# Four steps of an attention stage issued at other units: reciprocal sums, mask ranks, weight shifts, v loads

## The chip, the cores and the metric

One core of one Trainium2 chip. The metric is device time of the whole program in microseconds (us), the median of several runs. One execution was also recorded by the hardware profiler; all rows below come from that one. The engines are TensorE (PE), VectorE (DVE), ScalarE (ACT), GpSimd (POOL) and SyncE (SP), which here only issues DMAs.

## The reference

Three layers in a chain: clustered attention over 2 x 8 heads of 768 tokens with 64 dimensions, then a 512-2048-512 layer with a rational activation over 1536 tokens, then a 512-1024-512 layer with h * softmax(h) and a layer norm.

```python
q_assign = argmax(q_n @ c_n);  k_assign = argmax(k_n @ c_n)        # 16 clusters per head
scores = where(q_assign == k_assign, scale * q @ k.T, -1e9)
attn = softmax(scores);  x = attn @ v                               # heads side by side
h = x @ w_in;   P = a0 + a1*h + a2*h2 + a3*h3;   Q = 1 + |b0||h| + |b1|h2
x = (P / (Q + 1e-6)) @ w_out
h = x @ w2_in;  solu = h * softmax(h);  out = layernorm(solu) * g_ln @ w2_out
```

The weights arrive as 64-bit floats, whose two words the kernel turns into 32-bit floats itself.

## The kernel before

**Units.** The attention runs over 16 heads (n = 0 to 15) of six units each (t = 0 to 5), 96 units in all; a unit is 128 queries against 768 keys. `unit_scores` puts the scores in one of two PSUM tiles (two pairs of matmuls, L370 with q1/k1, L376 with q2/k2, the second carrying low parts and 16 mask rows). `unit_max` reduces them on VectorE (L381), `unit_exp` takes the exponential on ScalarE (L394), and every second unit `turn_p` transposes two units' probabilities on VectorE (L411). `pv_step` (L421) multiplies them with v one head later, 64 matmuls in each of the units t = 3, 4, 5. So a unit's scores can start only when the exponential of the unit two before has freed its PSUM tile.

**Beside the units** go four kinds of work, each cut into steps that the loop issues at chosen units:

- `prep_head(n+1)` on GpSimd: five operations (L324 three times, L338, L343) that split q and k of the next head, and two DMAs that copy its mask rows (L347, L348).
- `assign` for sets 2, 3 and 4 of heads: similarities on TensorE (L243), a copy on ScalarE (L252), then eight steps: `to_token` (L286), `top` (L290), `is_top` (L294), `rank` on GpSimd (L269), `top`, `is_top`, `from_token` (L297), `mask_out` (L304). The table `TCH` gives their units counted from `AT` = 5, 27, 50.
- `w1_f32`: ten half tiles of weights are turned from 64-bit to 32-bit, each a DMA (L116), a scaling on ScalarE (L126), a shift on VectorE (L127) and a shift-and-or on VectorE (L129), spread over units 28 to 87. This text calls one such half tile a conversion.
- for each pair of heads, `pair_sums` (the reciprocal of the sums, written to DRAM as rd, L463, and read back spread over partitions as rb, L466) and `pair_fin` on GpSimd (one add, L473, and two products with rb, L487).

All DMA issues named here stand in one queue, SyncE's, in one order; a DMA that waits holds those behind it. `load_head(n+2)`, called in the first unit of head n, loads q and k of a later head (dup) and its v. The v tile has two buffers, and v of head n+2 takes the one of head n, which `pv_step` reads in head n+1.

**The order on each engine** is not the order of the Python calls: the tile framework's scheduler sets it from those calls and its own timing estimates, so a moved call can move neighbours too. On each engine instructions then run in that order.

Of the kernel before, what the change touches and what calls it, by code (L numbers as in the profile page):

```python
# [15 lines left out]
B, H, S, D = 2, 8, 768, 64  # L16
# [14 lines left out]
def fused_kernel(ctx: ExitStack, tc: tile.TileContext, qT, kT, v, cent, w1, w2i, w2o, gln, coef, centT, cst, out):  # L31
# [20 lines left out]
    def psum1(name):  # L52
# [35 lines left out]
    S1A, S1B = 3, 7  # L88
    AT = (0, 0, 5, 27, 50)
    TCH = {  # L90
# [3 lines left out]
    }  # L94

    OLAG = 2
# [14 lines left out]

    def to_f32(w, src, nm):
        raw = cv[0].tile([128, 512], mybir.dt.uint64, name=f"raw{nm}", tag="raw")
        nc.sync.dma_start(out=raw, in_=src)  # L116
        yield
        words = raw.bitcast(U32).rearrange("p (n two) -> p n two", two=2)
        lo, hi = words[:, :, 0], words[:, :, 1]
        wf, wu = w, w.bitcast(U32)  # L120

        nc.scalar.activation(out=wf, in_=hi.bitcast(F32), func=AF.Prelu, scale=2.0 ** -112, alpha=-(2.0 ** 32))  # L126
        nc.vector.tensor_scalar(wu, wu, 3, None, op0=ALU.logical_shift_left)  # L127
        yield
        nc.vector.scalar_tensor_tensor(wu, lo, 29, wu, op0=ALU.logical_shift_right, op1=ALU.bitwise_or)  # L129
        yield  # L130
# [5 lines left out]
    w1_f, w1_t = {}, {}  # L136

    def w1_f32(f):
        w1_f[f] = wl0.tile([128, 1024], F32, name=f"w1f{f}", tag="l")
        for a in range(2):  # L140
            o = slice(512 * a, 512 * a + 512)
            yield from to_f32(w1_f[f][:, o], w1[f, :, o], f"w1{f}{a}")

    def w1_parts(f):
        h = wh["l" if f in (0, 12) else "r" if f < 5 or f > 12 else "m"].tile([128, 1024], F32R, name=f"w1h{f}", tag="h")
# [10 lines left out]
            yield  # L156


    raw = {}
    last = {}  # L160

    def load_pairs(es, parts=1):
# [12 lines left out]
    def load_head(n):  # L175
        b, h = divmod(n, H)
        for i, src in enumerate((qT, kT)):
            t = qk.tile([128, S], F32, name=f"dup{n}{i}", tag=f"dup{i}", bufs=2)
            if n:
                nc.sync.dma_start(out=t[0:64], in_=src[b, h])  # L180
            nc.sync.dma_start(out=t[64:128], in_=src[b, h])
            raw["d", n, i] = t

        t = qk.tile([128, S // 32, D], F32, name=f"v{n}", tag="v", bufs=2)
        for r in range(4):
            nc.sync.dma_start(out=t[32 * r:32 * r + 32], in_=v[b, h])
        raw["v", n] = t


    sets = [[(0, 0), (0, 1)], [(1, 0), (1, 1)], [(2, 0), (3, 0), (2, 1), (3, 1)], [(4, 0), (5, 0), (4, 1), (5, 1)], [(6, 0), (7, 0), (6, 1), (7, 1)]]  # L190
# [7 lines left out]
    t = psum4("warm")  # L198
# [108 lines left out]
    NB = 2  # L307
    q1 = [None] * NB
    q2, k1, k2 = [None] * NB, [None] * NB, [None] * NB
    vv = {}  # L310
    for i in range(NB):
        q1[i] = qk.tile([128, S], F32R, name=f"q1{i}", tag=f"q1{i}", bufs=1)
        q2[i] = qk.tile([128, S], F32R, name=f"q2{i}", tag=f"q2{i}", bufs=1)
# [16 lines left out]
    def prep_head(n, er=None, es=None):  # L330
        er = er or nc.gpsimd
        es = es or nc.gpsimd
        b, h = divmod(n, H)
        i = n % NB
        a, c, w = raw.pop(("d", n, 0)), raw.pop(("d", n, 1)), raw.pop(("v", n))
        rnd(er, k1[i], c, sgn[:, 1:2])
        yield
        es.tensor_tensor(k2[i][0:64], c[0:64], k1[i][0:64].bitcast(F32), op=ALU.subtract)  # L338
        yield
        rnd(er, q1[i], a, sgn[:, 0:1])  # L340
        rnd(er, q2[i][0:64], a[0:64], -0.125)
        yield
        es.tensor_tensor(q1[i][64:128], a[64:128], q1[i][64:128].bitcast(F32), op=ALU.subtract)  # L343
        yield
        if n:
            assert masked[next(k for k, es in enumerate(sets) if (n // 2, 0) in es)] == S
            nc.sync.dma_start(out=q2[i][64:80].bitcast(F32), in_=mk.pop((n, 0)).bitcast(F32))  # L347
            nc.sync.dma_start(out=k2[i][64:80].bitcast(F32), in_=mk.pop((n, 1)).bitcast(F32))  # L348
        yield
        vv[n] = w  # L350

# [10 lines left out]
    def unit_scores(n, t):  # L362
        i = n % NB
        sp = psum2("s", f"s{n}_{t}")
        sl = slice(t * 128, (t + 1) * 128)
        before = None
        for f in pre.pop(n * NT + t, ()):
            before = f(sp) or before
        for a in range(2):
            r = nc.tensor.matmul(sp[:, a, 0:384], lhsT=q1[i][:, sl], rhs=k1[i][:, a * 384:(a + 1) * 384], start=True, stop=False)  # L370
            if a == 0:
                last["pe0"] = r
            if before:
                behind(r, before)
        for a in range(2):
            last["pe"] = nc.tensor.matmul(sp[:, a, 0:384], lhsT=q2[i][:, sl], rhs=k2[i][:, a * 384:(a + 1) * 384], start=False, stop=True)  # L376
        return sp
# [114 lines left out]
    plan, planc, planp = ([[] for _ in range(97)] for _ in range(3))  # L492

    def spread(gen, n, i0, i1, plan=plan):
        for i in range(n):
            plan[min(96, i0 + (i1 - i0) * i // n)].append(gen)
# [5 lines left out]
    def run_plan(i):  # L502
        with tc.issue_after(last["pe"].ins) if i < 6 else ExitStack():
            for g in plan[i]:
                next(g, None)
        for h, p in ((("dve", "act"), planc), (("act",), planp)):
            with ExitStack() as es:
                for e in h:
                    es.enter_context(tc.issue_after(last[e].ins))
                for g in p[i]:  # L510
                    next(g, None)
# [24 lines left out]
    for i, (x1, x2, er) in enumerate(((q1[0], q2[0], nc.gpsimd), (k1[0], k2[0], nc.vector))):  # L536
        c, x = raw["p", 0, i], raw.pop(("d", 0, i))
# [4 lines left out]
        else:  # L542
            rnd(er, x2[0:64], c[0:64], -0.125)
            er.tensor_tensor(x1[64:128], x[64:128], x1[64:128].bitcast(F32), op=ALU.subtract)
    vv[0] = raw.pop(("v", 0))
    sps = [psum2("s", f"sim0{a}") for a in range(2)]
    for a in range(2):
        sims(0, 3 * a, 3, sps[a][:, 0, 0:384])
# [19 lines left out]
    for a in range(2):  # L568
        c = slice(384 * a, 384 * a + 384)
        nc.scalar.activation(out=q2[0][64:80, c], in_=ts[a][0:16, 0:384], func=AF.Identity, scale=-BIG, bias=big[0:16])  # L570
    for a in (1, 0):
        c = slice(384 * a, 384 * a + 384)
        nc.vector.tensor_copy(k2[0][64:80, c], ts[a][32 * jk:32 * jk + 16, 0:384])  # L573
    for a in range(2):
        c = slice(384 * a, 384 * a + 384)
# [39 lines left out]
    for idx, (n, t) in enumerate(units):  # L615
        if idx == ACL:
            asg.close()
            wh["r"] = ctx.enter_context(tc.tile_pool(name="wh2", bufs=4, side="right"))
        for k in range(3, len(sets)):
            if idx == AT[k] - LD:  # L620
                load_pairs(sets[k])
        if t == 0:
            if n + 2 < B * H:
                load_head(n + 2)
            if n >= 1 and n + 1 < B * H:
                spread(prep_head(n + 1), 7, idx, idx + 6)
        sp = unit_scores(n, t)
        m = unit_max(n, t, sp)
        if t % 2 and idx > 1:
            turn_p(*divmod(idx // 2 - 1, NT // 2))  # L630
        if idx == S1A:
            set1_a()
        if idx == S1B:
            set1_b()

        if n and t >= 3:
            for i in range(4 * (t - 3), 4 * (t - 2)):
                pv_step(n - 1, i)
            if t == 5 and n % 2 == 0:
                pair_sums(n // 2 - 1)  # L640
        unit_exp(n, t, sp, m)
        if n >= 2 and t < 2:
            pv_out(n - 2, t)
            if t == 1 and n % 2:
                spread(pair_fin(n // 2 - 1), 8, idx + 1, idx + 5)
        run_plan(idx)
    for i in range(2):
        pv_out(B * H - 2, i)
# [9 lines left out]
        pass  # L658
    for _ in pair_fin(B * H // 2 - 1):
        pass  # L660
    run_plan(96)
    pvs.close()
    ps["t"] = [e.enter_context(tc.tile_pool(name=f"pt{i}", bufs=1, space=PSUM, side=("left", "right")[i])) for i, e in enumerate(pt)]
    att.close()
# [316 lines left out]
```

## Time and profile before

| | |
|---|---|
| median of 3 runs | 718.29 us (716.08 to 720.64) |
| profiled execution | 716.94 us, span 714.8 us |
| TensorE busy | 618.5 us, 87% of the span |
| VectorE busy | 523.7 us, 73% |
| ScalarE busy | 410.0 us, 57% |
| GpSimd busy | 399.5 us, 56% |
| first score reduction / last unit's reciprocal (L447) | 22.42 us / 265.53 us |

The attention stage is about the first 266 us of the span, the two dense layers the rest. Shares over the whole span average over these stages, so the attention stage is read in its own rows. Row times are us from the start of the span; "x2" joins neighbours of a kind; in brackets stands how long the engine had been idle and what ended that.

### The profile page before, as it was taken

The numbers are of one execution on the slowest core, as the hardware profiler recorded it, in microseconds if no ns is written. First come the engines' busy times: TensorE is split into PE (matmuls) and PEld (weight loads), VectorE is DVE, ScalarE is ACT, GpSimd is POOL, SyncE is SP. The second block draws the span as 40 slices with busy tenths as digits, with TensorE's granted clock in tenths as the row PEclk, the third lists the DMA queues.
The fourth block names the chain that finished last, engine by engine and source line by source line (L and its number), as shares of the span: only waits on it lengthen the run. The fifth ranks groups of instructions, "written<-read, shape, count | busy, mean of one in ns | idle before, by whom it ended". The sixth has DMA issues, their size and how long they took to land.

```text
span 714.8 us, 13794 instructions
## 1 busy us (share of the span) xinstructions
PE 618.5 (87%) x5517; PEld 488.8 (68%) x5517; DVE 523.7 (73%) x695; ACT 410.0 (57%) x748; POOL 399.5 (56%) x363
## 2 busy tenths in 40 slices
PE   6668886587688869599999999889979999999998
PEld 3446665365566647477788878677858788888887
DVE  4497885979988783999866999987677865454450
ACT  1455654555666663787756877758557535443341
POOL 5464475554939753999865999997669600000000
PEclk7779999699878989899999999999999999999999
DMA  9963476746476224433100234330010000000001
GB/s 215 250 173 93 121 172 185 182 150 156 142 185 143 73 69 149 130 107 113 65 1 0 70 117 130 97 117 2 0 31 0 1 1 15 30 30 15 16 30 44
DMA packets 22439, 64.71 MB, mean 91 GB/s; under 512 B 4532, under 2 KB 5640, under 8 KB 22376
## 3 DMA queue, kind: packets, MB, share of 16 engines
q1 hardware_dynamic: 21944, 63.67, 32.0%
q8 instruction: 43, 0.70, 0.4%
q10 hardware_dynamic: 432, 0.17, 0.1%
q14 instruction: 20, 0.16, 0.1%
HBM read 59.16 MB, written 3.19 MB: 87 GB/s over the span
## 4 chain that ended last, share of the span: by engine, by line
PE 32%; DVE 13%; POOL 8%; issue 5%; ACT 3%; DMA 1%; POOLq 0%; ACTq 0%; DVEq 0%
PE hh L837 9%; PE o L888 9%; PE y L761 7%; PE h L709 4%; POOL q L725 2%; DVE w1w L129 2%; POOL gl L744 2%; DVE y L726 2%; POOL q L724 2%; DVE q L736 2%; DVE h L737 2%; PE lt L870 1%; DVE y L738 1%; DVE y L727 1%; DVE w1w L127 1%
## 5 line engine op out<-in xcount | busy, mean ns | idle before, releaser
L709 PE MATMUL h<-xhl,w1h 128*128 128x512 f32 x384 | 124.8, 402 | 20.4 <-DVE y L738 16.9
L394 ACT ACTIVATE p<-s,m 128x768 f32<-128x768 f32 x96 | 86.1, 899 | 80.5 <-DVE m L381 80.3
L370 PE MATMUL s<-k,q 128*128 128x384 f32 x192 | 65.9, 430 | 50.8 <-ACT p L394 50.2
L381 DVE TENSOR_REDUCE m<-s 128x1 f32<-128x768 f32 x96 | 89.1, 943 | 27.1 <-PE s L376 27.1
L709 PEld LDWEIGHTS h<-xhl,w1h 128*128 128x128 f32 x384 | 72.8, 192 | 40.9 <-DVE y L738 20.3
L411 DVE STREAM_TRANSPOSE pt<-p 128x1536 f32<-128x1536 f32 x48 | 84.5, 1762 | 0.0
L370 PEld LDWEIGHTS s<-k,q 128*128 128x128 f32 x192 | 34.5, 217 | 73.2 <-ACT p L394 54.8
L421 PE MATMUL pv<-pt,v 32*64 32x192 f32 x3072 | 83.7, 356 | 0.8 <-issue 0.8
L761 PE MATMUL y<-gl,w1h 128*128 128x512 f32 x192 | 75.7, 394 | 1.9 <-POOL gl L744 1.9
L421 PEld LDWEIGHTS pv<-pt,v 32*64 32x64 f32 x3072 | 65.1, 146 | 17.2 <-issue 10.2
L709 PE MATMUL h<-xhl,w1l 128*128 128x512 f32 x192 | 75.8, 396 | 0.0
L761 PE MATMUL y<-gh,w1l 128*128 128x512 f32 x192 | 75.0, 391 | 0.0
L744 POOL TENSOR_TENSOR gl<-y,gh 128x512 fp32r<-128x512 f32 x48 | 67.6, 1408 | 11.9 <-ACT gh L743 11.9
L761 PE MATMUL y<-gh,w1h 128*128 128x512 f32 x192 | 68.8, 393 | 0.2 <-ACT yp L777 0.2
L725 POOL TENSOR_TENSOR q<-q,t 128x512 f32<-128x512 f32 x48 | 67.5, 1405 | 2.6
L724 POOL TENSOR_SCALAR q<-t,ab 128x512 f32<-128x512 f32 x48 | 48.7, 1015 | 26.9 <-ACT t L722 18.2
L376 PE MATMUL s<-k,q 128*128 128x384 f32 x192 | 58.1, 390 | 1.5 <-DVE k L573 1.5
L726 DVE TENSOR_TENSOR y<-y,h 128x512 f32<-128x512 f32 x48 | 32.7, 681 | 30.0 <-ACT y L723 29.9
L733 ACT ACTIVATE h<-q,qc 128x512 f32<-128x512 f32 x48 | 33.1, 691 | 37.1 <-POOL q L725 27.9
L837 PE MATMUL hh<-vh,xhl 128*128 128x512 f32 x192 | 53.5, 392 | 1.0 <-ACT y L723 1.0
L487 POOL TENSOR_TENSOR xf<-u,rb 128x512 f32<-128x512 f32 (+1 forms) x14 | 14.3, 1044 | 64.6 <-DMA rb<-rd 64.6
L761 PEld LDWEIGHTS y<-gl,w1h 128*128 128x128 f32 x192 | 36.0, 188 | 11.3 <-POOL gl L744 3.6
(151 smaller groups left out, 1354.8 us busy)
## 6 DMA issues: line engine op xcount, KB each, us to landing
raww<-in_w SPq DMA_DIRECT2D x32, 512.0 KB, 3.2
v<-in_v SPq DMA_DIRECT2D x64, 192.0 KB, 5.0
dup<-in_qT SPq DMA_DIRECT2D x31, 192.0 KB, 4.6
dup<-in_kT SPq DMA_DIRECT2D x31, 192.0 KB, 3.5
rawv<-in_w2i SPq DMA_DIRECT2D x8, 512.0 KB, 4.0
rawv<-in_w2o SPq DMA_DIRECT2D x8, 512.0 KB, 4.2
out<-ob SPq DMA_DIRECT2D x11, 256.0 KB, 2.0
pr<-in_qT SPq DMA_DIRECT2D x7, 384.0 KB, 7.1
```

What stands on the lines that cost most here:

```text
L370: r = nc.tensor.matmul(sp[:, a, 0:384], lhsT=q1[i][:, sl], rhs=k1[i][:, a * 384:(a + 1) * 384], start=True, stop=False)
L381: last["dve"] = nc.vector.tensor_reduce(m, sp[:, :, 0:384], axis=AX.XY, op=ALU.min)
L394: last["act"] = nc.scalar.activation(out=P[n, t // 2][:, t % 2], in_=sp[:, :, 0:384], func=AF.Exp, scale=-1.0, bias=m, accum_out=rs[key][: ...
L411: r = nc.vector.transpose(PT[n][:, 2 * i:2 * i + 2].rearrange("p t k -> p (t k)"), p.rearrange("p t a k -> p (t a k)"))
L421: last["pv"] = nc.tensor.matmul(pv[n][64 * c:64 * c + 64, r, 0:192].rearrange("p (t q) -> p t q", t=NT), lhsT=vv[n][sl, j], rhs=PT[n][sl, ...
L709: r = nc.tensor.matmul(hp, lhsT=w[:, kt * 128:(kt + 1) * 128], rhs=x[:, kt], start=(i == 0), stop=(i == 11))
L724: nc.gpsimd.tensor_scalar(q, t, ab[:, 1:2], ab[:, 0:1], op0=ALU.mult, op1=ALU.add)
L725: nc.gpsimd.tensor_tensor(q, q, t, op=ALU.mult)
L744: nc.gpsimd.tensor_tensor(gl, y, gh.bitcast(F32), op=ALU.subtract)
L761: nc.tensor.matmul(o, lhsT=w[:, c], rhs=g, start=(first and i == 0), stop=(last and i == 2))
L837: last["th"] = nc.tensor.matmul(hp[:, a], lhsT=y[:, kt], rhs=w[:, 512 * a:512 * a + 512], start=(kt == 0 and e == 0), stop=(kt == 3 and e ...
L888: r = nc.tensor.matmul(op[:, 0:m], lhsT=l[:, kt], rhs=w, start=(n == 0), stop=(n == 23))
```

## The change

Four edits to the attention stage's issue points. The arithmetic is unchanged.

```diff
     TCH = {
-        2: (0, 1, 2, 4, 5, 6, 7, 10, 11, 12, 13),
-        3: (0, 2, 4, 6, 7, 8, 9, 12, 13, 14, 15),
+        2: (0, 1, 2, 3, 4, 5, 6, 10, 11, 12, 13),
+        3: (0, 1, 2, 3, 5, 6, 7, 12, 13, 14, 15),
...
-    def to_f32(w, src, nm):
+    def to_f32(w, src, nm, early=False):
...
         nc.scalar.activation(out=wf, in_=hi.bitcast(F32), func=AF.Prelu, scale=2.0 ** -112, alpha=-(2.0 ** 32))
+        if early:
+            yield
         nc.vector.tensor_scalar(wu, wu, 3, None, op0=ALU.logical_shift_left)
...
-            yield from to_f32(w1_f[f][:, o], w1[f, :, o], f"w1{f}{a}")
+            yield from to_f32(w1_f[f][:, o], w1[f, :, o], f"w1{f}{a}", True)
...
+    def load_v(n):
+
+        b, h = divmod(n, H)
         t = qk.tile([128, S // 32, D], F32, name=f"v{n}", tag="v", bufs=2)
         for r in range(4):
             nc.sync.dma_start(out=t[32 * r:32 * r + 32], in_=v[b, h])
-        raw["v", n] = t
+        vv[n] = t
...
+        if t == 2:
+            load_v(n)
         sp = unit_scores(n, t)
...
             if t == 1 and n % 2:
-                spread(pair_fin(n // 2 - 1), 8, idx + 1, idx + 5)
+
+                fin_ = pair_fin(n // 2 - 1)
+                for i in (1, 5, 6, 7):
+                    plan[min(96, idx + i)].append(fin_)
...
-    run_plan(96)
+    for _ in range(3):
+        run_plan(96)
```

Set 4 has the same row as set 3. The similarities are the first three numbers of a row, the eight steps the rest.

Three places of the built program. **SyncE's queue early in head 5**, where the sums of heads 2 and 3 travel (rt1, rd1, rb1; v5 is head 5's v, pr60 to pr71 are similarity inputs of heads 12 to 15, raww a weight half tile, q21 and k21 with oh2 mask rows). Before:

```order
L186 DMA v5_779<-in_v 32x1536 x4
L463 DMA rd1_1165<-rt1_1163 12x128
L171 DMA pr60_1463<-in_qT 128x768
L171 DMA pr70_1464<-in_qT 128x768
L466 DMA rb1_1167<-rd1_1165 64x768 x2
L171 DMA pr61_1465<-in_kT 128x768
L171 DMA pr71_1466<-in_kT 128x768
L116 DMA raww110_1514<-in_w1 128x512
L347 DMA q21_160<-oh2_369 16x768
L348 DMA k21_162<-oh2_369 16x768
```

and now:

```order
L191 DMA v5_1203<-in_v 32x1536 x2
L466 DMA rd1_1164<-rt1_1162 12x128
L191 DMA v5_1203<-in_v 32x1536 x2
L469 DMA rb1_1166<-rd1_1164 64x768 x2
L116 DMA raww110_1504<-in_w1 128x512
L351 DMA q21_155<-oh2_359 16x768
L352 DMA k21_157<-oh2_359 16x768
```

Two of the four loads of v5 now stand behind rd1, and the similarity inputs stand ahead of this piece. In both orders the four loads of dup8 (head 8) stand directly ahead of it. At the start of the queue the eight loads of v0 and v1 have moved behind the inputs of sets 1 and 2 and the small coef load. With it ScalarE's one operation that reads coef (L680), before behind the first two exponentials, now stands ahead of them.

**GpSimd in heads 5 and 6**, from the add of pair 1 (heads 2 and 3) to the rank of set 3 (e3) and the preparation of head 7 (k11, q11, q21, k21). Before:

```order
L473 TENSOR_TENSOR u1_970<-u1_970,w1_971 128x768
L487 TENSOR_TENSOR xf0_165<-u1_970,rb1_1167 128x512
L487 TENSOR_TENSOR xf1_166<-u1_970,rb1_1167 128x256
L324 TENSOR_SCALAR k11_161<-dup71_1176,sgn_83 128x768
L324 TENSOR_SCALAR q11_159<-dup70_1173,sgn_83 128x768
L324 TENSOR_SCALAR q21_160<-dup70_1173 64x768
L338 TENSOR_TENSOR k21_162<-dup71_1176,k11_161 64x768
L343 TENSOR_TENSOR q11_159<-dup70_1173,q11_159 64x768
L269 TENSOR_TENSOR e3_1027<-e3_1027,cst_70 128x768
```

and now:

```order
L476 TENSOR_TENSOR u1_953<-u1_953,w1_954 128x768
L490 TENSOR_TENSOR xf0_160<-u1_953,rb1_1166 128x512
L490 TENSOR_TENSOR xf1_161<-u1_953,rb1_1166 128x256
L274 TENSOR_TENSOR e3_1017<-e3_1017,cst_70 128x768
L328 TENSOR_SCALAR k11_156<-dup71_1174,sgn_83 128x768
```

The rank has moved ahead of the preparation of head 7. The two products still follow their add directly.

**VectorE in head 13** (m13_t is the reduction of unit t, w1f4 a weight tile). Before:

```order
L381 TENSOR_REDUCE m13_1_2781<-s13_1_2776 128x1
L411 STREAM_TRANSPOSE pt12_2612<-p12_4_2693 128x1536
L129 SCALAR_TENSOR_TENSOR w1f4_2695<-raww140_2696,w1f4_2695 128x512
L381 TENSOR_REDUCE m13_2_2794<-s13_2_2789 128x1
L381 TENSOR_REDUCE m13_3_2812<-s13_3_2807 128x1
L411 STREAM_TRANSPOSE pt13_2814<-p13_0_2771 128x1536
L381 TENSOR_REDUCE m13_4_2858<-s13_4_2853 128x1
L127 TENSOR_SCALAR w1f4_2695<-w1f4_2695 128x512
L381 TENSOR_REDUCE m13_5_2903<-s13_5_2898 128x1
L411 STREAM_TRANSPOSE pt13_2814<-p13_2_2796 128x1536
L129 SCALAR_TENSOR_TENSOR w1f4_2695<-raww141_2801,w1f4_2695 128x512
```

and now:

```order
L384 TENSOR_REDUCE m13_0_2753<-s13_0_2748 128x1
L384 TENSOR_REDUCE m13_1_2765<-s13_1_2760 128x1
L414 STREAM_TRANSPOSE pt12_2602<-p12_4_2683 128x1536
L129 TENSOR_SCALAR w1f4_2685<-w1f4_2685 128x512
L384 TENSOR_REDUCE m13_2_2783<-s13_2_2778 128x1
L131 SCALAR_TENSOR_TENSOR w1f4_2685<-raww140_2686,w1f4_2685 128x512
L384 TENSOR_REDUCE m13_3_2799<-s13_3_2794 128x1
L414 STREAM_TRANSPOSE pt13_2801<-p13_0_2755 128x1536
L384 TENSOR_REDUCE m13_4_2844<-s13_4_2839 128x1
L384 TENSOR_REDUCE m13_5_2889<-s13_5_2884 128x1
L414 STREAM_TRANSPOSE pt13_2801<-p13_2_2785 128x1536
```

One conversion's two operations stand in the head now, both between the reductions of units 1 and 3; none is left between units 4 and 5 or behind the last transpose. The same holds for most heads from 5 to 14, one conversion in each.

## Rows read from the trace of the kernel before

**Rows 1.** Windows: length, busy PE, PEld, DVE, ACT, POOL (count), clock, DMA share, GB/s.

```profile
0.00:20.00 20.00, 13.05 (x48) 6.72 (x48) 7.17 (x23) 4.38 (x8) 11.94 (x26) 0.74 0.94 217
...
180.00:240.00 60.00, 45.94 (x867) 35.59 (x868) 53.18 (x54) 38.17 (x75) 42.84 (x34) 0.86 0.62 155
```

**Rows 2.** Page, DMA issues: out<-in, queue, operation, count, KB each, us to landing.

```profile
v<-in_v SPq DMA_DIRECT2D x64, 192.0 KB, 5.0
```

**Rows 3.** Waits: engine, line, releaser: us in total, times, longest.

```profile
POOL xf L487 <- DMA rb<-rd: 64.6, 7, 12.4
```

**Rows 4.** Timeline of VectorE, head 14: start, us, line, operation [idle before].

```profile
237.92 1.75 DVE L381 TENSOR_REDUCE m<-s 128x1 f32<-128x768 f32 x2
...
241.52 0.96 DVE L381 TENSOR_REDUCE m<-s 128x1 f32<-128x768 f32 x1 [0.17 <-PE s L376]
242.98 0.96 DVE L381 TENSOR_REDUCE m<-s 128x1 f32<-128x768 f32 x1 [0.50 <-PE s L376]
...
247.95 0.96 DVE L381 TENSOR_REDUCE m<-s 128x1 f32<-128x768 f32 x1 [1.42 <-PE s L376]
...
250.52 1.78 DVE L381 TENSOR_REDUCE m<-s 128x1 f32<-128x768 f32 x2
```

**Rows 5.** Timeline of VectorE, heads 12 and 13: start of 12, two conversion steps of 13.

```profile
210.01 1.75 DVE L381 TENSOR_REDUCE m<-s 128x1 f32<-128x768 f32 x2
...
234.31 0.43 DVE L127 TENSOR_SCALAR w1f<-w1f 128x512 uint32<-128x512 uint32 x1 [1.68 <-ACT w1f L126]
...
237.21 0.65 DVE L129 SCALAR_TENSOR_TENSOR w1f<-raww,w1f 128x512 uint32<-128x512 uint32 x1
```

**Rows 6.** Timeline of ScalarE between heads 12 and 13, and at head 14.

```profile
222.01 0.67 ACT L126 ACTIVATE w1f<-raww 128x512 f32<-128x512 f32 x1
...
238.85 0.90 ACT L394 ACTIVATE p<-s,m 128x768 f32<-128x768 f32 x1 [0.35 <-DVE m L381]
```

**Rows 7.** Timeline of VectorE, head 6: its start, its wait, the next start.

```profile
112.80 1.75 DVE L381 TENSOR_REDUCE m<-s 128x1 f32<-128x768 f32 x2
...
125.64 0.95 DVE L290 TENSOR_REDUCE my<-e 128x48 f32<-128x768 f32 x1 [7.70 <-POOL e L269]
...
134.40 1.80 DVE L381 TENSOR_REDUCE m<-s 128x1 f32<-128x768 f32 x2
```

**Rows 8.** Timeline of GpSimd: products of pair 1, rank of set 3.

```profile
115.50 1.98 POOL L487 TENSOR_TENSOR xf<-u,rb 128x512 f32<-128x512 f32 x2 [12.41 <-DMA rb<-rd]
...
123.80 1.80 POOL L269 TENSOR_TENSOR e<-e,cst 128x768 f32<-128x768 f32 x1
```

**Rows 9.** Timeline of SyncE's queue: sums of pair 1 out and back.

```profile
104.11 0.34 SPq L463 DMA_DIRECT2D rd<-rt  x1
...
111.17 1.10 SPq L466 DMA_DIRECT2D rb<-rd  x2
```

**Rows 10.** Timelines of TensorE, ScalarE and VectorE, head 0 and before it.

```profile
11.91 0.56 PE L256 MATMUL set<-cst,sm 64*128 64x64 f32 x3 [1.54 <-DVE e L264]
14.89 4.03 PE L243 MATMUL sim<-pr,cT 128*32 128x384 f32 x8 [2.43 <-DMA pr<-in_qT]
...
29.31 0.20 ACT L680 ACTIVATE ab<-coef 128x2 f32<-128x2 f32 x1 [4.02 <-DMA coef<-in_coef]
...
32.13 0.96 DVE L381 TENSOR_REDUCE m<-s 128x1 f32<-128x768 f32 x1 [2.20 <-PE s L376]
```

**Rows 11.** Timelines of GpSimd and VectorE, a conversion step beside a GpSimd operation.

```profile
193.29 1.80 POOL L338 TENSOR_TENSOR k<-dup,k 64x768 fp32r<-64x768 f32 x1
...
193.30 2.08 DVE L127 TENSOR_SCALAR w1f<-w1f 128x512 uint32<-128x512 uint32 x1
```

**Rows 12.** Timelines of GpSimd and TensorE, start of head 11.

```profile
188.06 2.57 POOL L343 TENSOR_TENSOR q<-dup,q 64x768 fp32r<-64x768 f32 x1
...
191.38 0.60 PE L370 MATMUL s<-k,q 128*128 128x384 f32 x2
```

**Rows 13.** Timeline of TensorE, first dense layer: a wait and the row behind it.

```profile
533.32 1.06 PE L709 MATMUL h<-xhl,w1h 128*128 128x512 f32 x2 [4.75 <-DVE y L738]
```

More of the change, by code (lines that the diff above doesn't have):

```diff
@@ L156, in w1_parts @@
             yield
-    raw = {}
+    raw, vv = {}, {}
     last = {}
@@ L309, in fused_kernel @@
     q2, k1, k2 = [None] * NB, [None] * NB, [None] * NB
-    vv = {}
     for i in range(NB):
@@ L334, in prep_head @@
         i = n % NB
-        a, c, w = raw.pop(("d", n, 0)), raw.pop(("d", n, 1)), raw.pop(("v", n))
+        a, c = raw.pop(("d", n, 0)), raw.pop(("d", n, 1))
         rnd(er, k1[i], c, sgn[:, 1:2])
@@ L349, in prep_head @@
         yield
-        vv[n] = w
     XF = [xy.tile([128, 4, 512], F32, name=f"xf{j}", tag=f"xf{j}") for j in range(3)]
@@ L544, in fused_kernel @@
             er.tensor_tensor(x1[64:128], x[64:128], x1[64:128].bitcast(F32), op=ALU.subtract)
-    vv[0] = raw.pop(("v", 0))
     sps = [psum2("s", f"sim0{a}") for a in range(2)]
```

2 rows, old and new, of the table TCH are left out of this document.

## The prediction

> **What bounds the kernel now.** I read the windows first: between 180 and 240 us VectorE is busy 53.18 of 60 us, TensorE 45.94 at a granted clock of 0.86 [rows 1]. So in the attention stage VectorE is nearly the bound, and what counts is what makes it wait and what stands in its way between two heads. The list of waits comes next. Its longest on GpSimd is for rb, 64.6 us in seven waits [rows 3]; an idle GpSimd by itself costs nothing, so I looked for who waits behind it. Then I read VectorE's timeline head by head.
>
> Head 14 has no conversion and no set in it. It runs from 237.92 to 250.52, 12.60 us, with VectorE idle 0.17, 0.50 and 1.42 us before the reductions of units 2, 3 and 5 [rows 4], 2.09 together, each ended by TensorE's scores. There the chain of the head is TensorE's: unit 2's scores wait for unit 0's exponential, then three portions of PV stand between the scores of units 3, 4 and 5. Work that VectorE does between the reductions of units 1 and 5 fits into these 2.09 us; work after unit 5's reduction and before unit 1's of the next head lengthens the path in full.
>
> Heads 12 and 13 take 237.92 - 210.01 = 27.91 us [rows 4, 5], 2.71 more than twice 12.60, and hold two conversions: 1.35 us each, 13.5 for ten. The rows show where: the shift at 234.31 came 1.68 us after the previous work, waiting for ScalarE, directly ahead of unit 5's reduction, and the 0.65 us at 237.21 stands between the last transpose and the next head's first reduction [rows 5]. Both are places with no room.
>
> Head 6 takes 134.40 - 112.80 = 21.60 us, of which VectorE waits 7.70 for one thing, the rank of set 3 on GpSimd [rows 7]. That rank began at 123.80, after head 7's preparation, after products that had waited 12.41 us for rb [rows 8].
>
> **Part A, the queue at the start.** Eight v loads of 192 KB [rows 2] leave the front of SyncE's queue. At 217 GB/s in the first 20 us [rows 1], the four of v0 are 3.6 us, all eight 7.2. The similarities of set 1 began at 14.89 on arrival of their input [rows 10]; TensorE is free at 11.91 + 0.56 = 12.5, so they start 2.4 us earlier. Four score matmuls now stand between them and the mask transposes, about 1 us, so the first reduction comes 1.4 earlier. The coef load held ScalarE 4.02 us until 29.31 [rows 10], in the middle of head 0; at 22.1 it holds nobody for long, although L680 now stands ahead of the first exponential. Of these 4.02 VectorE saw 2.20 at unit 4 [rows 10]; I take 1.9. Against it, in head 1 the first `top` of set 2 now stands ahead of the step that releases set 1's mask, 0.95 by such a reduction [rows 7]. Together -1.4 - 1.9 + 0.9 = **-2.4**, between +1 (coef still late) and -5.4 (all of the 4.02).
>
> **Part B, the rank of set 3.** In the new order it follows the products directly; the five operations of head 7's preparation, which took it from 117.5 to 123.80 [rows 8], come after. rb1 comes sooner too: rd1 went out at 104.11 and rb1 only at 111.17, with two similarity inputs between [rows 9], which now stand ahead. So the rank ends at 119.3 at the latest (115.50 + 1.98 + 1.80, with rb unchanged), and some 3 us sooner if rb is; the reduction that reads it was ready at 117.9 (125.64 - 7.70). I take **-7.0**, between -6.3 (119.3 - 117.9 = 1.4 still waited) and -7.7. The four-unit gap before the products does not appear: the new order still has them directly behind their add, so most of the 64.6 us of GpSimd waiting stays. Two of four v loads moved behind rd1 are worth about 1 us per pair, no more.
>
> **Part C, the conversions.** The shift waits no longer, since its scaling is issued a unit earlier; shift and or (0.43 and 0.65 [rows 5], 1.08) lie between the reductions of units 1 and 4, inside the 2.09. What they add in full is ScalarE's: all ten scalings now stand between a head's last exponential and the next head's first. At 238.85 ScalarE waited only 0.35 for VectorE, with 0.65 of VectorE's late work in front [rows 5, 6], so without that work ScalarE is last there, and a scaling, 0.67 busy, costs most of itself: I take 0.6 [rows 6]. For blocking by GpSimd (below) I add 0.3. So 0.9 instead of 1.35 each, ten times: **-4.5**; between -13.5 (all hidden) and nothing.
>
> That blocking: the shift at 193.30 took 2.08 us instead of 0.43 while GpSimd's two-input operation ran from 193.29 for 1.80 [rows 11]. GpSimd runs five or six such operations of 1.8 us in two heads, 11 of 28 us: a chance of 0.4 times half a length, 0.36 an operation, 0.7 a conversion, of which 2.09 - 1.08 = 1.0 us of room swallows most. The Trainium skill, "SBUF — State Buffer", section "Who interferes with whom", speaks against putting more of this work beside a busier GpSimd: a VectorE operation of this kind and a GpSimd operation that reads SBUF exclude each other, and the later one waits for the whole of the other. The row agrees (1.65 us lost to 1.80). By that rule alone, every one of the 20 operations meeting GpSimd, part C would be the loss of the third rival below; by the shares of time in the rows it is the 0.3.
>
> **Part D, the rest.** Steps of sets 3 and 4 move between heads; one `to_token` now stands between head 5's first two reductions, where there is no room, and one behind head 8's last, while head 5's second `is_top` leaves such a place and head 9 holds less. Same instructions, so 0, with 1.75 (two reductions [rows 4]) either way. The preparation of odd heads comes closer: head 11's ended at 188.06 + 2.57 = 190.63, its scores began at 191.38 [rows 12], 0.75 us of room. If heads 9 and 10 shorten by two us and rb comes 1 us earlier, half a us is waited: **+0.5**. In the dense layers the order of the last units changes, the instructions do not: 0, up to +5 (fourth rival).
>
> **Sum.** -2.4 - 7.0 - 4.5 + 0.5 = -13.4 against the profiled execution's 716.94 us (span 714.8 and 2.1 around it): 703.5. The median of the runs shown is 1.35 above that execution, so I forecast **705**.
>
> **Rivals.**
>
> 1. *GpSimd's chain becomes the bound.* Preparation of an even head, its buffers' reload, v, rd, rb, products, preparation of the odd head: a loop, of which the 0.75 us at head 11 [rows 12] is the slack. For it: its waits hardly shrink. Against it: only head 11 was this close in what I read. If every pair is held to its old length, part C is lost: 705 + 4.5 = 709.5.
> 2. *The change does not do what it says.* The products' gap is already missing in the order. If rb also came no earlier and coef no sooner, parts A and D fail, B keeps 6.3 and C stands: 718.3 - 6.3 - 4.5 + 0.5 = 708.
> 3. *VectorE blocked by GpSimd in every conversion*, the slower case. Both operations blocked in full, 2 x 1.65 + 1.08 = 4.4, less 2.09 of room, plus 0.6: 2.9 a conversion against 1.35, so C is +15.5 instead of -4.5, and the time 705 + 20 = 725, slower than before by 7. It outweighs A and B from 2.7 us of blocking a conversion on (1.08 + 2.7 - 2.09 + 0.6 - 1.35 = 0.9, ten times 9). Against it: GpSimd's long waits stay, and the shares above give 0.7.
> 4. *A wait in the dense layers.* The last units of the first layer are interleaved more tightly; one more wait like that at 533.32, 4.75 us for VectorE [rows 13], would give 710. Against it: the new order also moves GpSimd's weight work behind these units' results.
>
> **How the numbers follow.** About 1% (7.2 us) is what this kernel's measurement can tell from no change. Chances: forecast 0.58, rival 1 0.15, rival 2 0.08, rival 3 0.06, rival 4 0.10, else 0.03. Faster by over 1% means below 711.1: forecast, rival 2, and part of rivals 1 and 4, whose times lie near that bound, 0.78. Within 1%: the rest of those and most of rival 3, 0.17. Slower: 0.05. The range runs from 698, where C saves half of its bound more and A all of its, to 713, where C or the dense layers give back as in rivals 1 and 4.
>
> **What would show it.** Head 6 near 14.5 us without the wait for the rank (B); ScalarE's L680 no longer waiting 4 us and the first score reduction near 21.0 instead of 22.42 (A); no shift ahead of unit 5's reductions and heads 7, 11 and 13 near 13.5 (C); GpSimd's wait for rb still over 45 us. The forecast is wrong if shifts of 1.5 us and more are common, if scores of odd heads wait for GpSimd, or if TensorE waits over 2 us in the last units of the first dense layer.

## The result, and the profile after

The changed kernel takes 709.54 us (708.25 to 711.83, four runs) against 718.22: a ratio of 0.9882 (0.9839 to 0.9924). Run again beside other experiments it gave 711.39 against 717.1, 0.9919 (0.9886 to 0.9952). So it is faster by 6 to 9 us, where 13 were forecast. Its profiled execution took 711.83 us, span 710.0.

The rows that answer to those of before. The start, in timelines of TensorE, ScalarE and VectorE [rows 10]:

```profile
10.90 3.38 PE L248 MATMUL sim<-pr,cT 128*32 128x384 f32 x8
...
19.36 0.19 ACT L688 ACTIVATE ab<-coef 128x2 f32<-128x2 f32 x1
...
19.21 1.82 DVE L384 TENSOR_REDUCE m<-s 128x1 f32<-128x768 f32 x2 [1.01 <-PE s L379]
...
31.91 0.94 DVE L384 TENSOR_REDUCE m<-s 128x1 f32<-128x768 f32 x1
```

Set 1's similarities start 3.99 earlier, the coef operation no longer waits, the first reduction comes at 19.21 instead of 22.42, and head 1 starts (the last row) at 31.91 instead of 37.53. Head 6 in VectorE's timeline, GpSimd's beside it [rows 7, 8], and SyncE's issues [rows 9]:

```profile
106.87 1.81 DVE L384 TENSOR_REDUCE m<-s 128x1 f32<-128x768 f32 x2
...
114.55 0.95 DVE L295 TENSOR_REDUCE my<-e 128x48 f32<-128x768 f32 x1 [2.14 <-POOL e L274]
...
117.11 2.30 DVE L131 SCALAR_TENSOR_TENSOR w1f<-raww,w1f 128x512 uint32<-128x512 uint32 x1
...
125.22 1.77 DVE L384 TENSOR_REDUCE m<-s 128x1 f32<-128x768 f32 x2
...
110.79 1.96 POOL L490 TENSOR_TENSOR xf<-u,rb 128x512 f32<-128x512 f32 x2 [13.69 <-DMA rb<-rd]
112.70 1.81 POOL L274 TENSOR_TENSOR e<-e,cst 128x768 f32<-128x768 f32 x1
...
117.04 1.81 POOL L342 TENSOR_TENSOR k<-dup,k 64x768 fp32r<-64x768 f32 x1
...
100.78 0.34 SPq L466 DMA_DIRECT2D rd<-rt  x1
...
105.84 1.73 SPq L469 DMA_DIRECT2D rb<-rd  x2
```

The rank stands right behind the products now, and VectorE waits 2.14 us for it instead of 7.70. Head 6 takes 18.35 us instead of 21.60, not the 14.5 forecast: besides the wait that is left it holds a conversion, whose or (its second operation, a shift-and-or) took 2.30 us. It began 0.07 after GpSimd's two-input operation at 117.04 and ended 0.56 after that one's end, which is about its own shortest time, 0.64. Then head 10, VectorE's timeline, with the longest loss of the changed kernel (18.71 us, before 15.23):

```profile
168.64 1.82 DVE L384 TENSOR_REDUCE m<-s 128x1 f32<-128x768 f32 x2 [0.51 <-PE s L379]
170.38 1.77 DVE L414 STREAM_TRANSPOSE pt<-p 128x1536 f32<-128x1536 f32 x1
172.07 1.35 DVE L129 TENSOR_SCALAR w1f<-w1f 128x512 uint32<-128x512 uint32 x1
...
175.80 0.95 DVE L295 TENSOR_REDUCE my<-e 128x48 f32<-128x768 f32 x1 [1.52 <-POOL e L274]
...
179.23 1.44 DVE L131 SCALAR_TENSOR_TENSOR w1f<-raww,w1f 128x512 uint32<-128x512 uint32 x1
180.59 2.55 DVE L299 TENSOR_TENSOR e<-e,my 128x768 f32<-128x768 f32 x1
```

Shift, or and `is_top` are 0.97, 0.80 and 1.63 above the shortest times of their kinds (0.38, 0.64 and 0.92), and the rank is waited for again (1.52, before not at all). In the views of windows, waits and TensorE's timeline [rows 1, 3, 13]:

```profile
0.00:20.00 20.00, 13.68 (x54) 7.64 (x55) 9.97 (x26) 6.28 (x12) 17.08 (x34) 0.88 0.94 257
...
180.00:240.00 60.00, 45.44 (x791) 34.29 (x774) 51.22 (x49) 37.38 (x73) 44.45 (x35) 0.80 0.60 153
...
POOL xf L490 <- DMA rb<-rd: 64.2, 7, 13.7
...
529.52 1.22 PE L717 MATMUL h<-xhl,w1h 128*128 128x512 f32 x2 [4.74 <-DVE y L746]
```

GpSimd's wait for rb is what it was (64.6 before), and so is the wait in the first dense layer (4.75).

The spans of all profiled executions, cut at three places of VectorE's timeline: the first score reduction, head 1's first, and the last reciprocal. "Pace" is a quarter of the time from pair 0's products on GpSimd to pair 4's, so the mean length of two heads as GpSimd sees it. "Conversions" is the sum of the twenty shifts and ors in the attention stage; at their shortest times they would take 10.2. The last two columns count heads 4 to 11: "heads wait" is what VectorE waits for a rank and TensorE's scores for a preparation, "GpSimd waits" what GpSimd waits, before a preparation or an add, for work of the heads. sp_alone has no row, since its profiled execution was a slow one (721.98 us against a median of 714.36).

| kernel | first reduction | head 1 | heads 1 to 15 | rest | pace | conversions | heads wait | GpSimd waits |
|---|---|---|---|---|---|---|---|---|
| before | 22.42 | 37.53 | 228.00 | 449.3 | 31.2 | 15.5 | 7.7 | 6.3 |
| changed | 19.21 | 31.91 | 227.67 | 450.4 | 30.7 | 18.7 | 3.7 | 1.7 |
| again | 21.47 | 34.29 | 227.29 | 448.2 | 30.4 | 21.3 | 0.7 | 4.8 |
| v_alone | 20.11 | 32.95 | 227.30 | 449.8 | 30.5 | 19.7 | 2.3 | 12.7 |
| rank_alone | 23.43 | 37.93 | 229.79 | 448.0 | 31.3 | 17.6 | 2.0 | 1.8 |
| shift_alone | 22.24 | 35.17 | 230.22 | 451.6 | 31.7 | 19.9 | 7.2 | 4.7 |
| no_early | 20.79 | 33.63 | 227.16 | 450.7 | 30.5 | 17.6 | 0 | 13.0 |
| combo | 18.23 | 32.63 | 223.64 | 449.7 | 30.5 | 20.4 | 0 | 4.7 |
| combo_rd | 20.12 | 32.96 | 224.57 | 449.5 | 30.4 | 21.4 | 0 | 16.0 |
| after_noconv | 21.49 | 34.16 | 227.12 | 448.2 | 31.4 | 0 | 13.6 | 1.2 |
| before_noconv | 20.66 | 33.54 | 230.14 | 449.6 | 31.8 | 0 | 13.4 | 5.1 |
| ops_back | 21.51 | 34.35 | 230.79 | 450.4 | 30.8 | 22.0 | 0 | 8.9 |
| after_odd | 19.60 | 32.44 | 221.68 | 448.2 | 29.3 | 13.1 | 3.9 | 1.5 |

The second and third rows tell the result: the start gained 5.6 and 3.2 us, heads 1 to 15 gained 0.3 and 0.7, where the forecast had 11. Single executions of one order differ: four of these kernels (before, rank_alone, shift_alone, before_noconv) start with the same instructions, and their head 1 begins between 33.5 and 37.9, in the mean at 36.0. In the nine that have the v edit it begins between 31.9 and 34.4, in the mean at 33.3. So before is a late one of its kind, and the start gained about 2.8 rather than 5.6. A term's size is read from the medians or from several rows, its place from these rows.

Where the 11 us went in heads 1 to 15 stands in VectorE's waits and in its busy time (the third number of a window's row), first before:

```profile
DVE m L381 <- PE s L376: 20.9, 26, 4.2
DVE my L290 <- POOL e L269: 7.7, 1, 7.7
DVE w1f L127 <- ACT w1f L126: 7.0, 6, 1.7
37.53:265.53 228.00, 174.24 (x3357) 132.75 (x3349) 192.29 (x186) 131.57 (x259) 134.53 (x125) 0.87 0.55 143
```

and now:

```profile
DVE m L384 <- PE s L379: 25.8, 21, 4.7
DVE my L295 <- POOL e L274: 3.7, 2, 2.1
31.91:259.58 227.67, 171.51 (x3357) 128.15 (x3349) 196.63 (x186) 131.23 (x259) 135.76 (x125) 0.89 0.57 147
```

The waits for the rank fell by 4.0 and those for scalings by 7.0, which is the 11 forecast. But VectorE waits 4.9 more for TensorE's scores, and its own operations take 4.3 more.

### The profile page after: what moved, and what is told of

It reads as the page before. It is cut to its first block, busy times and chain, and to the rows that moved or that the text cites. A ratio compares the mean times of both kernels' runs of the same rounds, so it can differ in the third digit from the quotient of the medians.

```text
span 710.0 us, 13783 instructions
## 1 busy us (share of the span) xinstructions
PE 617.8 (87%) x5517; PEld 487.6 (69%) x5517; DVE 528.8 (74%) x695; ACT 409.6 (58%) x748; POOL 399.5 (56%) x363
## 4 chain that ended last, share of the span: by engine, by line
PE 39%; DVE 13%; issue 4%; POOL 3%; ACT 2%; DMA 1%; SPq 0%; ACTq 0%; POOLq 0%; DVEq 0%
PE y L769 10%; PE o L896 9%; PE hh L845 9%; PE h L717 8%; DVE y L734 2%; DVE w1w L131 2%; DVE q L744 2%; DVE h L745 2%; PE lt L878 1%; DVE y L746 1%; DVE y L735 1%; DVE w1w L129 1%; DVE xhl L612 1%; POOL q L733 1%; DMA raww<-in_w 1%
## 5 line engine op out<-in xcount | busy, mean ns | idle before, releaser
L717 PE MATMUL h<-xhl,w1h 128*128 128x512 f32 x384 | 126.8, 406 | 20.5 <-DVE y L746 17.3
L373 PE MATMUL s<-k,q 128*128 128x384 f32 x192 | 63.8, 418 | 48.1 <-ACT p L397 47.6
L424 PE MATMUL pv<-pt,v 32*64 32x192 f32 x3072 | 86.8, 363 | 3.1 <-issue 2.9
L373 PEld LDWEIGHTS s<-k,q 128*128 128x128 f32 x192 | 33.1, 210 | 72.7 <-ACT p L397 55.2
L379 PE MATMUL s<-k,q 128*128 128x384 f32 x192 | 55.9, 378 | 2.3 <-DVE k L575 2.3
```

Source lines behind the costliest of these rows:

```text
L424: last["pv"] = nc.tensor.matmul(pv[n][64 * c:64 * c + 64, r, 0:192].rearrange("p (t q) -> p t q", t=NT), lhsT=vv[n][sl, j], rhs=PT[n][sl, ...
L717: r = nc.tensor.matmul(hp, lhsT=w[:, kt * 128:(kt + 1) * 128], rhs=x[:, kt], start=(i == 0), stop=(i == 11))
```

## Experiments

**The four edits one at a time.** The edit of `pair_fin` alone leaves every instruction of every engine in its place, so it was not run: the products already followed their add as closely as their data let them. The other three, each on the kernel before:

```diff
# v_alone (load_v as in the change)
+        if t == 2:
+            load_v(n)
```

> The kernel before with one edit: v is loaded in its own head. No VectorE row changes place; the queue's start does. Theory of the prediction (its part A): 2.4 us gained, near 716, the first score reduction at 21.0, and heads 1 to 15 as before. Theory from the trace of the changed kernel: the whole of its gain up to head 1 is this edit's, first score reduction at 19.2 instead of 22.42 and head 0 at 12.7 instead of 15.11, so 5 us gained, near 713; ScalarE's wait for coef is gone in both. Rival: the early gain is given back at head 2 or later, where v now comes 12 us later, and the time stays at 718.

714.63 us, ratio 0.9949 (0.9922 to 0.9976): 3.7 us, between the two forecasts of it. The start is the earlier one. In head 6 VectorE waits 2.28 instead of 7.70, with the rank still behind head 7's preparation: rd1 goes out at 98.81, and rb1 4.03 us behind it instead of 7.06. So this edit takes most of the wait that the rank edit was made to pay for.

```diff
# rank_alone
-        3: (0, 2, 4, 6, 7, 8, 9, 12, 13, 14, 15),
+        3: (0, 1, 2, 3, 5, 6, 7, 12, 13, 14, 15),
```

(sets 2 and 4 as in the change)

> The kernel before with one edit: the units of the steps of sets 2, 3 and 4. Theory of the prediction (part B): VectorE's 7.70 us wait for the rank in head 6 goes or shrinks to 1.4, and the time falls by 6.3 to 7.7, near 711. Theory from the trace of the changed kernel: the wait shrinks by 5.5 but only 3 us of it reach the end, because steps of set 4 now crowd head 10 (18.71 there instead of 15.23); 715 to 716, with head 10 above 17. Rival: nothing left at the end, 718, since the rank still waits for the products in front of it.

717.14, ratio 0.9988 (0.9963 to 1.0014): nothing. Yet head 6's wait for the rank is gone altogether, and it takes 14.31 instead of 21.60. Heads 4, 8 and 10 give most of it back: 16.56, 17.04 and 17.29 instead of 13.69, 15.50 and 15.23, together 6.5 us (in head 10 VectorE now waits 1.19 for that set's rank). TensorE's timeline in head 4:

```profile
87.06 0.62 PE L370 MATMUL s<-k,q 128*128 128x384 f32 x2 [1.84 <-ACT p L394]
...
87.98 0.65 PE L243 MATMUL s<-pr,cT 128*32 128x128 f32 x16
88.55 0.98 PE L370 MATMUL s<-k,q 128*128 128x384 f32 x2
89.32 0.84 PE L376 MATMUL s<-k,q 128*128 128x384 f32 x2
90.10 2.47 PE L421 MATMUL pv<-pt,v 32*64 32x192 f32 x64
92.50 0.65 PE L243 MATMUL s<-pr,cT 128*32 128x128 f32 x16
...
93.96 1.56 PE L421 MATMUL pv<-pt,v 32*64 32x192 f32 x64
95.45 0.65 PE L243 MATMUL s<-pr,cT 128*32 128x128 f32 x16
96.02 0.62 PE L370 MATMUL s<-k,q 128*128 128x384 f32 x2
```

All three similarities of set 3 now stand in units 3 to 5 of head 4, each with a portion of PV; before, the third was in head 5. It costs 0.57 (95.45 to 96.02). Behind an idle 1.84 a stretch ran at or near the lower of TensorE's two clock levels (1.2 GHz): PV took 2.47 instead of 1.56, scores 0.98 and 0.84 instead of 0.62 and 0.51; the granted clock from 84 to 102 us is 0.91, in the same head of before (83 to 98) 1.00, where TensorE idled 1.52 at the same place. Whether the packing made the clock fall is not shown. With the shift at this head's end, 1.49 instead of 0.77, that is 0.57 + 1.6 + 0.7 = 2.9 of 2.87.

```diff
# shift_alone
         nc.scalar.activation(out=wf, ...)
+        if early:
+            yield
         nc.vector.tensor_scalar(wu, wu, 3, ...)
```

> The kernel before with one edit: the shift is issued one unit behind its scaling. Theory of the prediction (part C): ten conversions at 0.9 instead of 1.35, 4.5 us gained, near 713.7; VectorE's 7.0 us of waits for scalings fall below 1. Theory from the trace of the changed kernel: those waits go, but shifts and ors meet GpSimd's operations more often (there 8.5 us above their shortest times instead of 5.3), and the time stays within 1.5 of 718. Rival, blocking dominates: 2 to 5 us slower, with shifts or ors of 1.3 us and more in at least eight of twenty.

720.03, ratio 1.0019 (0.9984 to 1.0054): no gain, and part C's -4.5 (0.9937) lies outside. The 7.0 us of waits for scalings are gone; the twenty operations take 19.9 instead of 15.5, eight of them 1.1 us or more. The edit also moves the second weight load and scaling of a tile to later places. no_early is the changed kernel without this edit:

> The changed kernel without its shift edit (each shift again directly behind its scaling). Theory of the prediction: 4.5 us slower than the changed kernel, near 714. Theory from its trace: the edit is worth nothing, 709 to 710. Rival, blocking dominates: without the edit it is 2 to 5 us faster, 705 to 707, and collisions in shifts and ors come to 5 us instead of 8.5.

714.34, ratio 0.9949 (0.9919 to 0.9979), where the changed kernel had 0.9882 and 0.9919. Taken with the first this looks like a gain of the shift edit, with the second, whose interval overlaps by more, like little or none. Unsettled; what is settled is that alone it brings nothing.

**The rank edit without its similarities.** again is the changed kernel; sp_alone and combo take the rank of set 3 forward and leave the similarities, and sets 2 and 4, at their old units.

```diff
# sp_alone, and with the v and shift edits combo
-        3: (0, 2, 4, 6, 7, 8, 9, 12, 13, 14, 15),
+        3: (0, 2, 4, 5, 6, 7, 8, 12, 13, 14, 15),
```

> The changed kernel itself once more, to have it beside the single edits. The single edits gave -3.7, -0.9 and +1.4 us, -3.2 together, and all but the shift edit -3.7; the changed kernel gave -8.7 in four runs. If the edits simply add, this one comes to 714 to 716; if the shift edit is worth more once the rank is out of the way, it stays at 709 to 711.

711.39, as said: between the two cases. The single edits add up to 3.2 us and the whole change to 5.7 or 8.7; whether the rest belongs to the edits together or to the scatter of runs (each interval is 3 us wide or more) stays open.

> The kernel before with one edit: the rank of set 3 one unit earlier, so that it stands ahead of head 7's preparation, with the similarities at their old units; nothing moves on TensorE. Theory 'similarities': the rank edit lost its 7 us because it packs similarities into the units in which TensorE has PV as well (heads 4 and 8, 2.9 and 2.4 us longer there); without that, head 6 keeps 14 to 15 us, heads 4 and 8 stay at 13.7 and 14.6, and the time is 711 to 713. Rival 'next limit': whatever head 6 saves, later heads give back, and the time is 716 to 718 with heads 7 to 10 longer by the same sum.

714.36, ratio 0.9933 (0.9898 to 0.9969), against 0.9988 for rank_alone. The intervals overlap by a little; the middle values put the packed similarities at 4 us, in line with heads 4 and 8 of rank_alone (2.9 and 1.5 longer than before).

> The kernel before with v in its own head, the shift edit, and the rank of set 3 one unit earlier with similarities at their old units. v alone left 2.28 us of head 6's wait, so the rank has only that to give here. If the shift edit is worth nothing: 711 to 713. If it is worth 4 us once nothing waits in head 6: 706 to 708. If the packed similarities had a use in the changed kernel, this one is slower than it.

709.01, ratio 0.9874 (0.9831 to 0.9918): as fast as the changed kernel or a little faster, head 6 without any wait at 15.01, heads 4 and 8 at 12.66 and 14.79.

**Is GpSimd's loop the bound?** combo_rd gives rb an earlier start:

```diff
# combo_rd
-        nc.sync.dma_start(out=d.rearrange(...), in_=rt)
+        nc.scalar.dma_start(out=d.rearrange(...), in_=rt)
```

> The kernel combo, with the small DMA that writes the reciprocal sums issued from ScalarE's queue, right behind the copy it reads, instead of SyncE's behind dup and v loads. rb can then follow the v loads at once: GpSimd's wait for it falls from 64 to 40 us or less. Theory 'GpSimd's chain' (rival 1 of the prediction): 2 to 4 us faster than combo. Rival: GpSimd's waits cost nothing any more, same as combo within 1 us; ScalarE's seven issues cost under 1 us.

710.18, ratio 0.9897 (0.9847 to 0.9947), the same as combo. From its list of waits:

```profile
POOL xf L490 <- DMA rb<-rd: 49.6, 7, 9.8
```

In combo it is 57.7; 40 or less was expected. From add to products pairs 1 to 4 take 10.4 us in the mean instead of 13.0, but from products to the next add 20.0 instead of 17.5, for GpSimd now waits there instead: before four preparations 4.19, 1.36, 3.93 and 5.56 us, where in combo it waits before two, 2.89 and 1.79. The profile names no releaser for these waits, but each of the preparations begins 0.16 us behind the last scores (L373) of the head whose buffer of k1 it writes anew. Here the scores end at 90.73:

```profile
90.11 0.62 PE L373 MATMUL s<-k,q 128*128 128x384 f32 x2
...
90.90 0.91 POOL L328 TENSOR_SCALAR k<-dup,sgn 128x768 fp32r<-128x768 f32 x1 [4.19 <-issue]
```

So GpSimd's loop is not closed in itself: each preparation waits for the heads. The pace cannot tell which of the two is the longer, since it is the mean length of two heads in either case (30.5 and 30.4 here). Who waits for whom can (the table's last columns). In combo and combo_rd the heads wait for GpSimd nowhere in heads 4 to 11, and GpSimd waits 4.7 and 16.0 us for the heads: the heads' own chain is the longer one, and a shorter way to rb only lengthens GpSimd's waits. In the changed kernel both columns are small, 3.7 and 1.7: there (and in again, 0.7 and 4.8) the two chains are about equally long.

The other side of this is what the conversions cost:

```diff
# before_noconv, after_noconv: for the five tiles of the attention stage
-        nc.vector.tensor_scalar(wu, wu, 3, ...)
-        nc.vector.scalar_tensor_tensor(wu, lo, 29, wu, ...)
```

> The kernel before without the same twenty operations (the same weights are left unfinished). Part C puts a conversion at 1.35 us there, of which at most 0.67 is the scaling's: 7 to 13.5 us faster than the kernel before, 705 to 711. If shifts and ors cost the same in both kernels, the two differences (this one and that of the changed kernel) agree within 2 us, and part C was worth nothing.

> The changed kernel without the shifts and ors of the ten conversions in the attention stage (their weights are left without the low words' bits); all else in the same order. The prediction's part C prices a conversion here at 0.9 us, of which 0.6 is ScalarE's scaling, which stays: 0.3 x 10 = 3 us faster than the changed kernel. Theory 'collisions': shifts and ors cost 0.8 us a conversion, 7 to 9 us faster, near 702.

719.88, ratio 1.0004 (0.9970 to 1.0037), and 711.54, ratio 0.9903 (0.9869 to 0.9936): without twenty operations, 15.5 and 18.7 us of VectorE's time, neither kernel is faster. The waits of before_noconv, then head 6 in its VectorE timeline, show where it goes:

```profile
DVE my L292 <- POOL e L271: 13.4, 2, 9.3
```

```profile
122.02 0.95 DVE L292 TENSOR_REDUCE my<-e 128x48 f32<-128x768 f32 x1 [9.30 <-POOL e L271]
```

In heads 1 to 15 VectorE is busy 179.9 and 180.2 us instead of 192.3 and 196.6, and waits the more: for the rank 13.4 and 8.4 instead of 7.7 and 3.7, for TensorE's scores 36.5 and 37.3 instead of 20.9 and 25.8. Both kernels have the heads waiting 13 us and more for GpSimd, so here its chain is the longer one. But they are not the same kernels less twenty operations: a load buffer comes free sooner, and the weight loads stand further ahead in SyncE's queue. In after_noconv one stands ahead of the transfers of dup, v and rd1, in the changed kernel behind rb1 (at 107.67):

```profile
97.36 0.33 SPq L116 DMA_DIRECT2D raww<-in_w  x1
...
110.77 1.10 SPq L471 DMA_DIRECT2D rb<-rd  x2
```

rb1 goes out 7.21 us behind rd1 there instead of 5.06, about the 2.27 by which head 6's wait for the rank grew. So the two runs show that a conversion's time on VectorE alone does not set the time; how much of what they failed to gain is due to the moved loads stays open.

**A place for the conversions.** after_odd puts both conversions of a tile between the reductions of units 2 and 5 of the odd head, where GpSimd waits for rb; nothing moves on TensorE or GpSimd.

```diff
# after_odd
-            yield from to_f32(w1_f[f][:, o], w1[f, :, o], f"w1{f}{a}", True)
+        g = [to_f32(w1_f[f][:, 512 * a:512 * a + 512], ..., True) for a in range(2)]
+        for a in (0, 1, 0, 1, 0, 0, 1, 1):
+            next(g[a])
+            yield
...
-        spread(w1_f32(f), 8, ...)
+        w1g = w1_f32(f)
+        for i in (0, 0, 1, 2, 4, 4, 5, 6):
+            planc[28 + 12 * f + i].append(w1g)
```

> The changed kernel with the shifts and ors of both halves of a weight tile moved into one odd head, between the reductions of units 2 and 5, where GpSimd waits for rb; nothing else moves on VectorE, nothing on TensorE or GpSimd. Theory 'collisions': there the twenty operations come near their shortest times, 10 to 12 us together instead of 18.7 to 21.3, heads 6, 8, 10, 12 and 14 are 1 to 2 us shorter each and the odd ones no longer than 1 us more: 3 to 6 us faster than the changed kernel, near 705. Rival 'room': collisions cost little since VectorE waits for TensorE anyway, same as the changed kernel within 1.5 us.

705.79, ratio 0.9817 (0.9782 to 0.9852): the fastest of all, 12.6 us below before. Head 7 in VectorE's timeline:

```profile
129.49 0.42 DVE L129 TENSOR_SCALAR w1f<-w1f 128x512 uint32<-128x512 uint32 x1
...
132.63 0.39 DVE L129 TENSOR_SCALAR w1f<-w1f 128x512 uint32<-128x512 uint32 x1
132.93 0.68 DVE L131 SCALAR_TENSOR_TENSOR w1f<-raww,w1f 128x512 uint32<-128x512 uint32 x1
133.53 0.95 DVE L385 TENSOR_REDUCE m<-s 128x1 f32<-128x768 f32 x1
134.40 0.68 DVE L131 SCALAR_TENSOR_TENSOR w1f<-raww,w1f 128x512 uint32<-128x512 uint32 x1
135.95 0.96 DVE L385 TENSOR_REDUCE m<-s 128x1 f32<-128x768 f32 x1 [0.88 <-PE s L380]
```

Two conversions in one head, and it takes 13.86; the twenty operations take 13.1 together. Heads 6, 8 and 10 take 14.63, 14.06 and 14.63 (18.35, 14.24 and 18.71 in the changed kernel), heads 1 to 15 221.68, the pace is 29.3. In heads 1 to 15 VectorE is busy 189.9 us, 6.8 less than in the changed kernel, and these heads are 6.0 shorter. The waits in both directions stay small (3.9 and 1.5), so heads' chain and GpSimd's became shorter together; in after_noconv, which did without these operations, the heads waited 13.6 us for GpSimd. TensorE's granted clock is not the cause: in heads 1 to 15 it is 0.89 here and in the changed kernel, and 0.86 in again, where these heads are as long as in the changed kernel.

With the conversions, after_odd also moves five scalings and four weight loads. The last run moves the scalings alone:

```diff
# ops_back: as after_odd, but
-        for i in (0, 0, 1, 2, 4, 4, 5, 6):
+        for i in (0, 0, 1, 2, 3, 4, 9, 10):
```

> The changed kernel with the second scaling of each weight tile on ScalarE moved from behind the last exponential of an odd head to between its first two exponentials, as in after_odd; the shifts and ors stay in their heads as in the changed kernel (three of them change places with one neighbour), the loads too. Theory 'seam': the scaling between two heads is what costs (part C: 0.6 each), five moved away give 3 us or more, and most of what after_odd won is here: 706 to 708. Theory 'collisions on GpSimd': after_odd won because shifts and ors beside GpSimd's preparation slow the loop of preparation, loads, rb and products; here they still do, and the time is that of the changed kernel, 709 to 711, with shifts and ors at 17 us or more together.

715.69, ratio 0.9958 (0.9930 to 0.9986): slower than the changed kernel, which neither theory had. ScalarE's timeline in head 7:

```profile
131.88 0.66 ACT L126 ACTIVATE w1f<-raww 128x512 f32<-128x512 f32 x1 [2.42 <-DMA raww<-in_w]
132.44 0.89 ACT L398 ACTIVATE p<-s,m 128x768 f32<-128x768 f32 x1
```

The scaling came ahead of its weight load, and the head's second exponential waited behind it, three times (in heads 7, 11 and 13) and 5.9 us in all. If each of these microseconds counted in full, 715.7 less 5.9 would be 709.8, the changed kernel's time, and nothing would be left for a scaling taken from the seam of two heads; that is an estimate. The run shows that after_odd's gain needs the loads or the shifts and ors moved as well; which of the two does it stays open.

## Why the prediction came out as it did

The time lay inside the range, and the sum was 4.5 us too optimistic. Its terms did worse than that: of the 11 us for heads 1 to 15 the two profiles show 0.3 and 0.7.

- **Part A**, -2.4: right in mechanism, and in size as far as the runs can tell. The coef operation no longer waits (in combo it still waited 2.06) and the first reduction comes earlier, as written. Over the thirteen rows the v edit is worth 2.8 us up to head 1, and set 1's similarities start 2.6 earlier in the mean; the 3.99 of the two profiles is a matter of single executions. v_alone's 3.7 (1.7 to 5.6) holds something else besides: rb1 comes sooner, which took 5.4 us of head 6's wait. "Worth about 1 us per pair, no more" was too low for pair 1 (from rd1 to rb1 7.06 before, 4.03 in v_alone, 5.06 in the changed kernel).
- **Part B**, -7.0: the place was right, the step from there to the end was wrong. Head 6's wait fell to 2.14 (0.67 in again) and to 0 in rank_alone, and the time did not follow. The step that failed is "same instructions, so 0" in part D: it counted VectorE's reductions and left out that the edit packs similarities on TensorE into the units of PV, and that set 4's rank is then waited for in head 10. rank_alone's heads 4, 8 and 10 are 6.5 us longer together; sp_alone, without the packing, gained 4.8 (2.2 to 7.3).
- **Part C**, -4.5: wrong. VectorE's waits for scalings went, 7.0 us, as forecast; longer operations (4.3, of which the conversions 3.2) and more waiting for scores (4.9) took their place. The estimate of 0.7 us of blocking a conversion was near (18.7 and 21.3 us are 0.85 and 1.1 above the shortest). The step that failed is that room of 2.09 us a head would swallow most of it. That room was read in head 14, which has no set; in heads 6 and 10 of the changed kernel the steps of a set stand in it, inside them VectorE idles for nothing but the rank (2.14 and 1.52), and `is_top`, for which no blocking was priced, is blocked too (2.55 instead of 0.92). Heads 7, 11 and 13, forecast near 13.5, take 14.99, 15.45 and 14.31. Without the twenty operations no time was gained, so neither 1.35 nor 0.9 holds as a price by itself.
- **Part D**: +0.5 for odd heads does not show, since no scores wait for a preparation in the changed kernel; dense layers 449.3 before, 450.4 and 448.2 after, nothing.
- **Rival 1** (709.5) has the measured time, but not the mechanism: that they agree is luck. It held every pair to its old length by GpSimd's loop. In the changed kernel the heads wait for GpSimd 3.7 us, in again 0.7, and in combo, which is as fast, not at all; and the long wait for rb could shrink from 57.7 to 49.6 us in combo_rd without a gain. What it had right is that GpSimd's chain is near: the heads wait 13 us and more for it in the two kernels without the conversions.
- **Rival 2** was right on one edit, that of `pair_fin`, and wrong on coef and rb.
- **Rival 3** (725): the blocking is real, in 8 of 20 operations with 1.2 us and more, just the share of 0.4 that was taken; its turning point of 2.7 us a conversion is far away. The rule cited from the Trainium skill, "SBUF — State Buffer", section "Who interferes with whom", that the later of the two waits for the whole of the other, agrees with the or at 117.11: 1.66 lost to an operation of 1.81.
- **Rival 4**: no new wait; 4.74 stands where 4.75 stood.

## What to carry to other kernels

Before a removed wait is booked, ask which chain is the longer one behind it. The time from one step's start to the same step's next start does not tell, since two chains that wait for each other show the same; count instead how long each waits for the other. Shortening the one that waits brings nothing (combo_rd). Room for more work is read in the heads that will hold it, not in the emptiest one. Here moving small work into the time in which the other engine waits for a transfer shortened both chains. And a table of units moves steps on every engine that they use: count each.

## What the runs showed of the hardware

VectorE and GpSimd held each other up in both directions. The or of 2.30 us ended at 119.41, 0.48 into GpSimd's next two-input operation, which took 2.13 instead of 1.81. `is_top` began inside that one, took 1.68 instead of 0.92 and ended at 121.88; GpSimd's one-input operation that began at 121.16 took 1.49 instead of 0.91. So an operation of VectorE in the wrong place also lengthens GpSimd's preparation:

```profile
118.93 2.13 POOL L347 TENSOR_TENSOR q<-dup,q 64x768 fp32r<-64x768 f32 x1
...
120.20 1.68 DVE L299 TENSOR_TENSOR e<-e,my 128x768 f32<-128x768 f32 x1
...
121.16 1.49 POOL L328 TENSOR_SCALAR k<-dup,sgn 128x768 fp32r<-128x768 f32 x1
```
